# Five y pairs prepared in the key sweep, gates on GpSimd, and three more MLP steps by seven products

## Chip, core, metric

The kernel runs on one core of a Trainium2 chip. The metric is device time in microseconds (us) of one execution. The engines are named as in the profile: PE (TensorE matmuls), PEld (its weight loads), DVE (VectorE), ACT (ScalarE), POOL (GpSimd), SP (SyncE, which here only issues DMAs).

## The reference, cut to what matters

```python
# x: 2048 x 576, 32 heads of 18, F = 4608
g = sigmoid((x * gate_w).sum(-1, keepdims=True))
q, k, v = split(x @ wqkv);  phi = where(t > 0, t + 1, exp(t)) + 1e-6
a = ((phi(q) @ (phi(k)^T v)) / (phi(q) . sum(phi(k)) + 1e-6)) @ wo      # linear attention
y = layernorm(x);  b = gelu(y @ w1 + b1) @ w2 + b2                      # MLP, tanh gelu
out = g * a + (1 - g) * b
```

## The kernel before

All products run in fp32r: an operand is kept as a rounded high part (an ACT copy) and a low residue (a DVE subtraction), and two or three of the products of these parts are accumulated in PSUM.

**Key sweep.** Tokens are cut into 16 tiles of 128. For each tile the sweep forms keys and queries, their feature maps, and adds to the sum of keys times x. Each tile has three numbered moments, 3n, 3n+1 and 3n+2, at which listed jobs are put into the engines' queues; "step 16" below is such a moment. Jobs run in the order written, engine by engine. The gates (`gates_in`, `gates_act`, `gates_out`) turn a few columns of sums into sigmoid and 1/sqrt(variance); `share_moments` stores mean and 1/sqrt for later broadcast by a DMA that POOL issues. A *y pair* is the MLP's input for two tiles, laid out for the seven-product scheme: `load_pair` (SP) reads moments and transposed x, `normal_pair` and `sum_pair` (DVE) normalise and combine, `split_pair` (ACT, DVE) rounds seven parts, `store_pair` (SP) writes them to DRAM. The table `Y_JOBS` says at which step each is put. Four pairs, all of the first token half, are made in the sweep, and the four of the second half later, during the MLP, by `make_y`.

**Middle.** `project_values(t)` makes five row blocks of the weight `wp` on PE; each is copied by ACT and its residue made by DVE. `normalize(i, ...)` divides the queries of tile i (part 0: reduction and reciprocal, part 1: one scaling on DVE), `tail_q` copies their tail on ACT. Then `attend` handles the 16 tiles.

**MLP.** 36 steps: 18 chunks of w1 and w2 for the first token half (k = 0 to 17), then 18 for the second. The *up* part of a step is seven products of seven matmuls of 512 columns, tile `ps<-y,wa` or `ps<-y,wb`. The *down* part, tile `ps<-region,h`, comes one step later in two forms. Plain (`plain_unit`): 8 units of 12 matmuls of 288 columns, 96 in all. By seven products (`one_of_seven`, steps in the set `SEVEN`): 14 units of 6 matmuls, 84 in all, for which sums of w2's quarters (tile `fresh`, 4 of 288 columns) and of h (tile `u`, 4 of 512 columns) are needed, on DVE or POOL by the set `ON_DVE`, and more rounding of both. A step that is also in `FIVES` keeps one product in a buffer of its own, which takes copies by ACT and fewer additions by DVE than a step that is in `SEVEN` alone. In the first half w1 must be summed and rounded too, and the y pairs be made; the second half reads w1's rounded parts back.

A planner at the end of the program lists all these operations with costs and due times, and writes them out engine by engine; `TUNED` holds its parameters, `HEAR` what it adds for the time from one engine to another. Its numbers order the instructions and no more.

```python
def sum_w2(n, eng):
    to, x0, x1 = ((T3, B22, B12), (T1, B12, B11), (T2, B22, T1), (T4, B21, T2))[n]
    eng.tensor_tensor(out=of(to), in0=of(x0), in1=of(x1), op=OP.subtract)
```

Of the kernel before, what the change touches and what calls it, by code (L numbers as in the profile page):

```python
# [33 lines left out]
MOMENTS = ((0, 2), (2, 4), (4, 6), (6, 8), (8, 16))  # L34
# [42 lines left out]
Y_JOBS = ((13, (16, 16, 17, 17), (18, 18, 19, 19), (18, 19, 20, 21)), (20, (22, 22, 23, 23), (25, 25, 27, 27), (25, 26, 28, 29)), (27, (31, 31, 32, 32), (33, 33, 34, 34), (34, 35, 35, 36)), (35, (37, 37, 38, 38), (39, 39, 41, 41), (40, 42, 43, 44)))  # L77
# [49 lines left out]
def tile_gated_mix(ctx: ExitStack, tc: tile.TileContext, x, xm, xe, wm, we, wvm, wve, wo, um, ue, w2, b1, b2, gw, out):  # L127
# [33 lines left out]
    dve.memset(ones, 1.0)  # L161
    tiny = keep.tile([P, 1], F32, name="tiny")
# [200 lines left out]
    def gates_in(b):  # L363
        own, ve, _, _ = gate_parts(b)
        dve.tensor_copy(mr[b][:, 0], nmean[:, own])
        dve.tensor_scalar(ve, sumsq[:, own], 1 / D, EPS_LN, op0=OP.mult, op1=OP.add)

        dve.tensor_scalar(g[:, own], gsum[:, own], -87.0, None, op0=OP.max)

    def gates_act(b):  # L370
        own, ve, _, rstd = gate_parts(b)
        act.activation(g[:, own], g[:, own], AF.Exp, scale=-1.0)
        act.activation(rstd, ve, AF.Sqrt)
        if MOMENTS[b][1] < NT:
            act.activation(tiny, ones[:, 0:1], AF.Exp)

    def gates_out(b):
        own, ve, vr, rstd = gate_parts(b)
        dve.tensor_scalar(g[:, own], g[:, own], 1.0, None, op0=OP.add)
        dve.reciprocal(g[:, own], g[:, own])  # L380
        dve.tensor_scalar(omg[:, own], g[:, own], -1.0, 1.0, op0=OP.mult, op1=OP.add)
        dve.reciprocal(rstd, rstd)

        dve.tensor_mul(vr, rstd, rstd)
        dve.tensor_mul(vr, vr, ve)
        dve.tensor_scalar(vr, vr, -0.5, 1.5, op0=OP.mult, op1=OP.add)
        dve.tensor_mul(rstd, rstd, vr)
# [43 lines left out]
    def split_pair(sup, j, part, stage, width=2):  # L431
# [4 lines left out]
        act.activation(to[:, :, 0:3], src, AF.Copy)  # L436
        dve.tensor_sub(to[:, :, 3:5], src[:, :, 0:2], raw(to[:, :, 0:2]))
# [123 lines left out]
    jobs = {n: [] for n in range(3 * NT)}  # L561
# [15 lines left out]
    for b, n in enumerate((9, 13, 22, 28)):  # L577
        at(n, gates_in, b)
        at(n + 1, gates_act, b)
        at(n + 2, gates_out, b)  # L580
        at(n + 2, share_moments, b)

    for j, (loaded, normal, added, parts) in enumerate(Y_JOBS):
# [3 lines left out]
        for m, when in enumerate(added):  # L587
            at(when, sum_pair, 0, j, m)
# [1055 lines left out]
```

## Time and profile before

| | us |
|---|---|
| median of 3 runs (lowest to highest) | 1095.16 (1095.01 to 1095.65) |
| the profiled execution, its own time | 1096.17 |
| its span, first to last instruction | 1094.5 |
| PE busy in it | 1086.3 (99%) |
| DVE busy | 922.4 (84%) |
| ACT busy | 691.3 (63%) |
| POOL busy | 236.2 (22%) |
| granted TensorE clock | 1.0 throughout |

The profile is of one execution. What lies between its time and its span (1.67 us) is outside the instructions. Busy shares are means over stages that differ: in the first half of the MLP, DVE is far busier than its mean.

### The profile page before, as it was taken

What the parts mean: (1) busy time and instruction counts of PE and PEld (TensorE: products, weight loads), DVE (VectorE), ACT (ScalarE), POOL (GpSimd) and SP (SyncE); (2) the same over time, 40 slices, a digit from 0 to 9 for tenths busy, and PEclk for the clock granted to TensorE, in tenths of its full rate; (3) what the DMA queues carried; (4) which work ended last, traced back from release to release, by engine and by line L of the source; (5) the groups of instructions that cost most, each with busy time, mean ns of one, the idle gap of its engine ahead of it and who ended that gap; (6) DMA issues with size and microseconds to landing.
All of it is one profiled execution on the core that took longest, in us unless ns stands there. A gap on an engine that the chain in (4) does not pass through costs nothing.

```text
span 1094.5 us, 18650 instructions
## 1 busy us (share of the span) xinstructions
PE 1086.3 (99%) x6712; PEld 996.6 (91%) x6712; DVE 922.4 (84%) x1558; ACT 691.3 (63%) x1235; POOL 236.2 (22%) x232
## 2 busy tenths in 40 slices
PE   9999999999999999999999999999999999999998
PEld 8999999999898889988889988989899999999898
DVE  4568786896799999899999997988887888878888
ACT  6677766454667887777877876455555555455552
POOL 2111113431123232332111202121122211221110
PEclk9999999999999999999999999999999999999999
DMA  6466772745745665764556559574444445444432
GB/s 179 135 87 190 172 218 101 278 178 191 249 156 188 196 203 185 239 209 169 194 184 220 191 197 396 170 252 118 135 148 118 130 119 148 131 122 118 133 102 87
DMA packets 109006, 189.72 MB, mean 173 GB/s; under 512 B 8940, under 2 KB 68604, under 8 KB 104818
## 3 DMA queue, kind: packets, MB, share of 16 engines
q1 hardware_dynamic: 108002, 187.78, 53.7%
q8 instruction: 53, 0.87, 0.3%
q10 hardware_dynamic: 720, 0.74, 0.2%
q14 instruction: 39, 0.32, 0.1%
q0 software_dynamic: 192, 0.01, 0.0%
HBM read 121.70 MB, written 66.80 MB: 172 GB/s over the span
## 4 chain that ended last, share of the span: by engine, by line
PE 92%; DVE 3%; DMA 3%; ACT 1%; issue 0%; SPq 0%; ACTq 0%; DVEq 0%
PE ps L120 92%; DVE accs L120 1%; DMA accs<-moments 1%; DMA yd<-ystage 1%; DMA s<-in_wm 0%; DVE h L120 0%; DMA ystage<-late_acc 0%; DMA fresh<-in_ue 0%; DMA s<-in_we 0%; DVE wa L120 0%; DVE region L120 0%; DVE ystage L120 0%; DVE wb L120 0%; DVE fresh L120 0%; ACT u L120 0%
## 5 line engine op out<-in xcount | busy, mean ns | idle before, releaser
L120 PEld LDWEIGHTS ps<-region,h 128*128 128x128 f32 x3072 | 437.5, 188 | 30.2 <-ACT ps L120 4.7
L120 PE MATMUL ps<-region,h 128*128 128x288 f32 x3072 | 456.8, 295 | 0.8 <-DVE accs L120 0.7
L120 DVE TENSOR_TENSOR accs<-ps,accs 128x576 f32<-128x576 f32 x330 | 246.1, 753 | 60.7 <-PE ps L120 53.9
L120 PE MATMUL ps<-y,wa 128*128 128x512 f32 x1008 | 257.6, 392 | 0.0
L120 PEld LDWEIGHTS ps<-y,wa 128*128 128x128 f32 x1008 | 180.8, 188 | 30.5 <-ACT ps L120 0.2
L120 POOL TENSOR_TENSOR fresh<-fresh 128x288 f32<-128x288 f32 (+1 forms) x128 | 117.1, 918 | 409.5 <-DVE accs L120 144.5
L120 PE MATMUL ps<-y,wb 128*128 128x512 f32 x756 | 199.2, 393 | 0.4 <-ACT u L120 0.4
L120 DVE TENSOR_TENSOR h<-u,h 128x512 fp32r<-128x512 f32 x240 | 165.4, 702 | 8.7 <-ACT u L120 8.7
L120 PEld LDWEIGHTS ps<-y,wb 128*128 128x128 f32 x756 | 133.8, 188 | 21.1 <-ACT u L120 0.6
L120 PE MATMUL ps<-y 128*128 128x288 f32 (+2 forms) x950 | 133.9, 297 | 2.2 <-DVE wp L120 1.1
L120 PEld LDWEIGHTS ps<-y 128*128 128x128 f32 (+1 forms) x950 | 129.8, 188 | 4.4 <-DVE wp L120 1.8
L120 ACT ACTIVATE region<-fresh 128x576 fp32r<-128x576 f32 (+1 forms) x132 | 81.2, 625 | 73.9 <-PE ps L120 73.3
L120 ACT ACTIVATE ps<-ps 128x576 f32<-128x576 f32 (+1 forms) x127 | 78.6, 621 | 45.0 <-PE ps L120 21.5
L120 POOL TENSOR_TENSOR u<-u 128x512 f32<-128x512 f32 x44 | 57.1, 1298 | 193.2 <-DVE h L120 54.8
L120 DVE TENSOR_TENSOR region<-fresh,region 128x576 fp32r<-128x576 f32 (+1 forms) x132 | 94.3, 727 | 1.1 <-ACT region L120 1.1
L120 ACT ACTIVATE u<-ps 128x512 f32<-128x512 f32 x73 | 43.0, 589 | 68.2 <-PE ps L120 68.2
L120 ACT ACTIVATE h<-u 128x512 fp32r<-128x512 f32 x128 | 73.4, 621 | 9.9 <-DVE u L120 5.5
L120 ACT ACTIVATE h<-u,b1s 128x512 fp32r<-128x512 f32 x73 | 52.6, 722 | 42.2 <-DVE u L120 42.1
L120 PE MATMUL ps<-wp,qt 128*128 128x288 f32 x448 | 63.0, 297 | 0.0
L120 DVE TENSOR_TENSOR u<-ps,u 128x512 f32<-128x512 f32 x74 | 50.4, 683 | 13.6 <-PE ps L120 12.7
L120 PEld LDWEIGHTS ps<-wp,qt 128*128 128x128 f32 x448 | 59.8, 188 | 0.0
L120 DVE TENSOR_TENSOR u<-u 128x512 f32<-128x512 f32 x84 | 58.0, 691 | 1.7 <-POOL u L120 1.1
(139 smaller groups left out, 1044.8 us busy)
## 6 DMA issues: line engine op xcount, KB each, us to landing
w1d<-wa SPq DMA_DIRECT2D x17, 1280.0 KB
wa<-w1d SPq DMA_DIRECT2D x68, 320.0 KB
fresh<-in_w SPq DMA_DIRECT2D x70, 288.0 KB
y<-yd SPq DMA_DIRECT2D x14, 1280.0 KB
w1d<-wb SPq DMA_DIRECT2D x17, 960.0 KB
wb<-w1d SPq DMA_DIRECT2D x51, 320.0 KB
yd<-ystage SPq DMA_DIRECT2D x28, 320.0 KB
fresh<-in_um SPq DMA_DIRECT2D x64, 128.0 KB
```

The costliest lines, as they stand in the source:

```text
L120: self.last = self.tc.keep_in_program_order(op(*args, **kwargs))
```

## The change

It makes the first pair of the second token half in the sweep as well, so that five pairs stand there, one every six steps, and `make_y` makes three; splits `split_pair` into a high and a low part with steps of their own; moves the gates' arithmetic from DVE to POOL, with powers in place of reciprocals and square root, so that ACT's only function there is Exp; puts steps 0, 6 and 13 into `SEVEN` (and 6, 13 and 17 into `FIVES`, 16 out of it); lets each sum of w1 and w2 choose its engine apart; changes the planner's costs and parameters; and issues tile 1's scaling and its tail behind the copy of wp's fourth row block.

```diff
-MOMENTS = ((0, 2), (2, 4), (4, 6), (6, 8), (8, 16))
+MOMENTS = ((0, 2), (2, 4), (4, 6), (6, 8), (8, 10), (10, 16))
...
-Y_JOBS = ((13, (16, 16, 17, 17), (18, 18, 19, 19), (18, 19, 20, 21)), (20, (22, 22, 23, 23), (25, 25, 27, 27), (25, 26, 28, 29)), (27, (31, 31, 32, 32), (33, 33, 34, 34), (34, 35, 35, 36)), (35, (37, 37, 38, 38), (39, 39, 41, 41), (40, 42, 43, 44)))
+Y_JOBS = ((9, 14, (16, 16, 17, 17), (18, 18, 19, 19), (18, 19, 19, 20), (19, 20, 20, 21)), (15, 20, (22, 22, 23, 23), (24, 24, 25, 25), (24, 25, 25, 26), (25, 26, 26, 27)), (21, 26, (28, 28, 29, 29), (30, 30, 31, 31), (30, 31, 31, 32), (31, 32, 32, 33)), (27, 32, (34, 34, 35, 35), (36, 36, 37, 37), (36, 37, 37, 38), (37, 38, 38, 39)), (33, 38, (40, 40, 41, 41), (42, 42, 43, 43), (42, 43, 43, 44), (43, 44, 44, 45)))
...
-SEVEN = set([1, 2, 3, 4, 5, 7, 8, 9, 10, 11, 12, 14, 15, 16, 17, 18, 19, 20, 21, 22, 23, 24, 25, 26, 27, 28, 29, 30, 31, 32, 33, 34])
+SEVEN = set([0, 1, 2, 3, 4, 5, 6, 7, 8, 9, 10, 11, 12, 13, 14, 15, 16, 17, 18, 19, 20, 21, 22, 23, 24, 25, 26, 27, 28, 29, 30, 31, 32, 33, 34])
...
-FIVES = set([1, 2, 3, 4, 5, 7, 8, 9, 10, 11, 12, 14, 15, 16])
+FIVES = set([1, 2, 3, 4, 5, 6, 7, 8, 9, 10, 11, 12, 13, 14, 15, 17])
...
+HEAR_NS = {"PE": 155, "ACT": 65, "DVE": 65, "POOL": 110, "DMA": 300}
...
     def gates_act(b):
-        own, ve, _, rstd = gate_parts(b)
+        own = gate_parts(b)[0]
         act.activation(g[:, own], g[:, own], AF.Exp, scale=-1.0)
-        act.activation(rstd, ve, AF.Sqrt)
-        if MOMENTS[b][1] < NT:
-            act.activation(tiny, ones[:, 0:1], AF.Exp)
 
     def gates_out(b):
         own, ve, vr, rstd = gate_parts(b)
-        dve.tensor_scalar(g[:, own], g[:, own], 1.0, None, op0=OP.add)
-        dve.reciprocal(g[:, own], g[:, own])
...
+        n = ve.shape[1]
+        pool.tensor_scalar(omg[:, own], g[:, own], 1.0, None, op0=OP.add)
+        pool.tensor_tensor(out=g[:, own], in0=omg[:, own], in1=powers[:, 0:1].to_broadcast([P, n]), op=OP.pow)
...
+        pool.tensor_tensor(out=rstd, in0=ve, in1=powers[:, 1:2].to_broadcast([P, n]), op=OP.pow)
...
-    for b, n in enumerate((9, 13, 22, 28)):
-        at(n, gates_in, b)
-        at(n + 1, gates_act, b)
-        at(n + 2, gates_out, b)
-        at(n + 2, share_moments, b)
...
+    for pair, (gated, loaded, normal, added, high, low) in enumerate(Y_JOBS):
+        sup, j = divmod(pair, TPB)
+        at(gated, gates_in, pair)
+        for step in (gates_act, gates_out, share_moments):
+            at(gated + 1, step, pair)
...
+        at(loaded, load_pair, sup, j)
...
     project_values(2)
+    project_values(3)
     normalize(1, (1,))
+    project_values(4)
     tail_q(1)
-    project_values(3)
-    project_values(4)
...
     def make_y():
...
-        for j in range(TPB):
+        for j in range(len(Y_JOBS) - TPB, TPB):
```

Three places show what moves. First PE at the start of the MLP, before: 49 up matmuls of step 0, then those of step 1 with step 0's down matmuls (`region,h`) among them.

```order
L120 MATMUL ps<-y,wa 128x512 x28
L120 MATMUL ps<-y,wb 128x512 x21
L120 MATMUL ps<-y,wa 128x512 x28
L120 MATMUL ps<-region,h 128x288 x12
L120 MATMUL ps<-y,wb 128x512 x7
L120 MATMUL ps<-region,h 128x288 x24
L120 MATMUL ps<-y,wb 128x512 x7
```

The same place in the change:

```order
L120 MATMUL ps<-y,wa 128x512 x28
L120 MATMUL ps<-y,wb 128x512 x21
L120 MATMUL ps<-y,wa 128x512 x25
L120 MATMUL ps<-region,h 128x288 x6
L120 MATMUL ps<-y,wa 128x512 x3
L120 MATMUL ps<-y,wb 128x512 x4
L120 MATMUL ps<-region,h 128x288 x6
```

Units of 6 stand where units of 12 stood. Over the program the matmuls of this tile go from 3072 to 3036, all others keep their number, and the stretches of up matmuls between down matmuls go from 298 to 285.

Second, DVE in the middle, before: `wp` residues are the row blocks, `accs<-accs,den` is the scaling of a tile's queries (the first here is tile 1's), `den` rows are part 0 of `normalize`.

```order
L120 TENSOR_TENSOR wp<-ps,wp 128x576 x2
L120 SCALAR_TENSOR_TENSOR accs<-accs,den 128x576
L120 TENSOR_TENSOR wp<-ps,wp 128x576 x2
L120 TENSOR_REDUCE den<-qz 128x32
L120 TENSOR_TENSOR den<-den,den_2182 128x32
```

In the change:

```order
L120 TENSOR_TENSOR wp<-ps,wp 128x576 x3
L120 SCALAR_TENSOR_TENSOR accs<-accs,den 128x576
L120 TENSOR_TENSOR wp<-ps,wp 128x576
L120 TENSOR_REDUCE den<-qz 128x32
L120 TENSOR_TENSOR den<-den,den_2238 128x32
```

The fourth block's residue now stands ahead of the scaling. On ACT five `wp` copies stand in a row, where three stood ahead of tile 1's tail and two behind.

Third, POOL in the sweep, before: `pks` is the running sum of the keys, the DMA stores a pair's moments.

```order
L120 TENSOR_TENSOR pks<-pks,k 128x576
L120 DMA moments_116<-mr_110 128x4x1
L120 TENSOR_TENSOR pks<-pks,k 128x576 x2
L120 DMA moments_117<-mr_111 128x4x1
L120 TENSOR_TENSOR pks<-pks,k 128x576 x3
```

In the change, the first pair's operations behind ACT's Exp and their DMA (three more, on mean, variance and gate sum, stand ahead of the Exp):

```order
L120 TENSOR_SCALAR omg<-g 128x2
L120 TENSOR_TENSOR g<-omg,powers 128x2
L120 TENSOR_TENSOR mt<-omg,g 128x2
L120 TENSOR_SCALAR mt<-mt 128x2
L120 TENSOR_TENSOR g<-g,mt 128x2
L120 TENSOR_SCALAR omg<-g 128x2
L120 TENSOR_TENSOR mr_113<-mt,powers 128x2
L120 TENSOR_TENSOR mt<-mr_113 128x2
L120 TENSOR_TENSOR mt<-mt 128x2
L120 TENSOR_SCALAR mt<-mt 128x2
L120 TENSOR_TENSOR mr_113<-mr_113,mt 128x2
L120 DMA moments_120<-mr_113 128x4x1
```

Fourteen small POOL operations per pair stand ahead of the DMA, eleven of them behind ACT's Exp.

From the end of attention to the first weighing of the first token half's output, the orders also count, before and in the change: DVE additions from PSUM into `accs` 133 and 140, residues of h 121 and 128, sums of w2 32 and 41, sums of h 36 and 40, residues of w2 66 and 72, sums of w1 28 and 32, merges of `ps` into `u` 40 and 39; POOL sums of h 20 and 28, of w2 20 and 27, of w1 36 and 32.

## Rows read from the trace of the kernel before

**Rows 1.** The page: busy time by engine, and the chain that ended last.
```profile
PE 1086.3 (99%) x6712; PEld 996.6 (91%) x6712; DVE 922.4 (84%) x1558; ACT 691.3 (63%) x1235; POOL 236.2 (22%) x232
...
PE 92%; DVE 3%; DMA 3%; ACT 1%; issue 0%; SPq 0%; ACTq 0%; DVEq 0%
```

**Rows 2.** Waits of PE: total us, times, longest us.
```profile
PE ps L120 <- DVE wp L120: 1.1, 1, 1.1
...
PE ps L120 <- DVE accs L120: 0.7, 1, 0.7
PE ps L120 <- ACT u L120: 0.4, 1, 0.4
```

**Rows 3.** Busy time by stretch: PE, PEld, DVE, ACT, POOL, clock, DMA, GB/s.
```profile
50.00:195.00 145.00, 145.00 (x976) 138.78 (x975) 107.63 (x236) 102.38 (x225) 26.00 (x20) 1.00 0.59 153
345.00:650.00 305.00, 304.50 (x1801) 273.18 (x1800) 292.67 (x495) 237.81 (x395) 75.78 (x70) 1.00 0.58 196
720.00:1090.00 370.00, 370.00 (x2219) 336.45 (x2220) 310.58 (x469) 195.20 (x322) 71.05 (x75) 1.00 0.44 130
```

**Rows 4.** Timeline of PE: a short and the longest stretch of down matmuls.
```profile
301.09 1.74 PE L120 MATMUL ps<-region,h 128*128 128x288 f32 x12
...
1076.35 14.43 PE L120 MATMUL ps<-region,h 128*128 128x288 f32 x108
```

**Rows 5.** Timelines of PE, ACT and DVE in the middle stage.
```profile
191.99 7.99 PE L120 MATMUL ps<-y 126*128 126x288 f32 x54
...
201.67 3.99 PE L120 MATMUL ps<-y 128*128 128x288 f32 x28 [1.14 <-DVE wp L120]
...
199.98 0.31 ACT L120 ACTIVATE tail<-accs 128x128 f32<-128x128 f32 x1 [2.00 <-DVE accs L120]
200.19 1.17 ACT L120 ACTIVATE wp<-ps 128x576 fp32r<-128x576 f32 x2
...
198.68 1.26 DVE L120 SCALAR_TENSOR_TENSOR accs<-accs,den 128x576 f32<-128x576 f32 x1
200.86 1.42 DVE L120 TENSOR_TENSOR wp<-ps,wp 128x576 fp32r<-128x576 f32 x2 [0.92 <-ACT wp L120]
```

**Rows 6.** Groups by form: busy us, mean ns, idle us before.
```profile
L120 DVE TENSOR_TENSOR accs<-ps,accs 128x576 f32<-128x576 f32 x330 | 246.1, 753 | 60.7 <-PE ps L120 53.9 <-ACT u L120 3.4
L120 DVE TENSOR_TENSOR h<-u,h 128x512 fp32r<-128x512 f32 x240 | 165.4, 702 | 8.7 <-ACT u L120 8.7
L120 POOL TENSOR_TENSOR fresh<-fresh 128x288 f32<-128x288 f32 x92 | 80.4, 874 | 307.0 <-DMA fresh<-in_w 113.7 <-DVE accs L120 112.5 <-DVE fresh L120 25.7
...
L120 POOL TENSOR_TENSOR u<-u 128x512 f32<-128x512 f32 x44 | 57.1, 1298 | 193.2 <-DVE h L120 54.8 <-ACT u L120 53.6 <-DVE accs L120 29.1
...
L120 DVE TENSOR_TENSOR accs<-accs 128x384 f32<-128x384 f32 x32 | 18.5, 577 | 0.3
...
L120 DVE TENSOR_TENSOR fresh<-fresh 128x288 f32<-128x288 f32 x32 | 15.4, 480 | 0.0
...
L120 DVE TENSOR_TENSOR ystage<-accs,ystage 128x256 fp32r<-128x256 f32 x28 | 11.8, 420 | 0.0
```

**Rows 7.** Tile fresh on POOL: duration ns min/median/max, first and last start.
```profile
L120 POOL TENSOR_TENSOR fresh<-fresh x128: 802/815/2951, 291.1 to 1046.0; 128x288 f32<-128x288 f32 x92, 128x384 f32<-128x384 f32 x36
```

**Rows 8.** Key sweep: timelines of SP, DVE, PE, POOL, and one DMA's landing.
```profile
62.95 0.34 SPq L120 DMA_DIRECT2D accs<-moments  x1
...
72.70 3.81 DVE L120 TENSOR_TENSOR accs<-accs 128x768 f32<-128x768 f32 x4
...
50.74 3.90 PE L120 MATMUL ps<-y 128*128 128x288 f32 x28
...
61.94 3.90 PE L120 MATMUL ps<-y 128*128 128x288 f32 x28
...
3.36 0.73 POOL L120 TENSOR_SCALAR_AFFINE_SELECT accs<-accs 126x126 f32<-126x126 f32 x2
...
moments<-mr POOLq DMA_DIRECT2D x4, 2.0 KB, 10.2
```

More of the change, by code (lines that the diff above doesn't have):

```diff
@@ L161, in tile_gated_mix @@
     dve.memset(ones, 1.0)
+    powers = keep.tile([P, 2], F32, name="powers")
+    pool.memset(powers[:, 0:1], -1.0)
+    pool.memset(powers[:, 1:2], -0.5)
     tiny = keep.tile([P, 1], F32, name="tiny")
@@ L429, in tile_gated_mix, with split_pair, high_pair @@
     ys = {}
-    def split_pair(sup, j, part, stage, width=2):
+    def split_pair(*args):
+        high_pair(*args)
+        low_pair(*args[:3])
+    def high_pair(sup, j, part, stage, width=2):
         m0, m1 = width * part, min(width * part + width, 7)
@@ L436, in split_pair, with low_pair @@
         act.activation(to[:, :, 0:3], src, AF.Copy)
+    def low_pair(sup, j, part):
+        _, _, src, to = ys[sup, j, part]
         dve.tensor_sub(to[:, :, 3:5], src[:, :, 0:2], raw(to[:, :, 0:2]))
@@ L558, in tile_gated_mix @@
     y_stages.append(y_place.rearrange("p (m s n) -> p m s n", m=2, s=5))
-    jobs = {n: [] for n in range(3 * NT)}
+    jobs = {n: [] for n in range(3 * NT + 3)}
     def at(n, f, *args):
@@ L576, in tile_gated_mix @@
     at(40, load_wo)
[L577 to L584 removed]
+    for pair, (gated, loaded, normal, added, high, low) in enumerate(Y_JOBS):
[3 more added lines that the diff above has]
+            at(gated + 1, step, pair)
         for n, when in enumerate(normal):
[L586 removed]
+            at(when, normal_pair, sup, j, n // 2, n % 2)
         for m, when in enumerate(added):
[L588 to L592 removed]
+            at(when, sum_pair, sup, j, m)
+        for part, when in enumerate(high):
+            at(when, high_pair, sup, j, part, lambda part=part: y_stages[part])
+        for part, when in enumerate(low):
+            at(when, low_pair, sup, j, part)
+            at(when, split_tails, sup, j, part)
+            at(min(when + 1, 3 * NT + 2), store_pair, sup, j, part)
+        at(loaded, load_pair, sup, j)
     def run(n):
@@ L647, in tile_gated_mix @@
     projected(late[0], QUERY)
+    run(3 * NT)
     queries_out(late[0])
@@ L650, in tile_gated_mix @@
     moments_of(end)
+    run(3 * NT + 1)
     for part in range(2):
         add_products(end, part)
+    run(3 * NT + 2)
     pz = [ps[:, 6 + half, :HALF] for half in range(2)]
@@ L909, in tile_gated_mix @@
     COST = {ACT: (91, 0.838, 97), DVE: (70, 1.0425, 84), POOL: (250, 2.19, -78)}
-    HEAR = {PE: 155, ACT: 33, DVE: 33, POOL: 78, DMA: 30}
+    HEAR = HEAR_NS
+    EACH = {"up": (226.8, (6.3, 9.3, -2.7, 4.3, 9.3, 1.5, 5.5, 4.2)), "down": (131.9, (0, 3, -1, -2, 7, 1, 2, 3, -6, 1, 0, 1))}
     class Op:
@@ L1051, in sum_on @@
     def sum_on(what, k, m=0):
-        own = ((what, k, m) in ON_DVE) != ((m, k < NCHUNK) in DVE_SUMS)
+        own = (what, k, m) in ON_DVE
         return (DVE, dve) if own else (POOL, pool)
@@ L1128, in make_w2 @@
             for n in range(4):
[L1129 removed]
+                engine, eng = sum_on("w2", k, n)
                 op(engine, lambda n=n, eng=eng: sum_w2(n, eng), HALF, needs=[("w2raw", k)] + ([("w2sum", k, n - 1)] if n else []),
@@ L1445, in tile_gated_mix, with plan @@
     assert len(in_order) == len(ops)
-    def plan(lag, late, slop, slack, guard, ahead, second=None):
-        second = second or (lag, late, slop, slack, guard, ahead)
+    def plan(lag, late, slop, slack, guard, ahead, second, hold, wait):
         slot, due = {o: n for n, o in enumerate(ups)}, {}
@@ L1471, in plan, with streams @@
         port_at, moved, landed = {e: 0 for e in port_until}, 0.0, []
-        next_up, next_down, shift = 0, 0, 0.0
+        next_up, next_down, shift, run = 0, 0, 0.0, ["", 0]
+        def streams(o):
+            n = round(o.ns / (231.7 if o.by[0] == "up" else 132.3))
+            each, more = EACH[o.by[0]]
+            at_ = run[1] if run[0] == o.by[0] else 0
+            return n, n * each + sum(more[at_:at_ + n])
         def offer(o):
@@ L1520, in choose @@
                     if ta is not None and tb is not None:
-                        if tb <= ta + 100:
+                        if tb <= ta + 100 and not (run[0] == "up" and run[1] < hold and behind < wait and ta <= free[PE]):
                             ta = None
@@ L1550, in plan @@
             s, _, o = min(picks, key=lambda x: x[:2])
-            e, t = o.engine, s + o.tail
+            e, t, ns = o.engine, s + o.tail, o.ns
             if e == PE:
+                n, ns = streams(o)
+                t += ns - o.ns
+                run[:] = o.by[0], n + (run[1] if run[0] == o.by[0] else 0)
                 shift = s - nominal[o]
@@ L1557, in plan @@
                         late, slop, slack, guard = second[1:5]
+                        hold, wait = second[6:8]
                 else:
@@ L1580, in plan @@
             else:
-                free[e] = s + o.ns
+                free[e] = s + ns
             if o.port:
```

34 lines of the change are left out of this document (14 added, 20 removed).

## The prediction

> **What bounds the kernel now.** I read the page first: PE is busy 99% of the span, and the chain that ended last is PE for 92% [rows 1]. A busy PE could still be a waiting one, so the waits of PE come next: they hold one wait of 1.1 us on the residue of `wp`, one of 0.7 on DVE's additions into `accs`, and one of 0.4 on an ACT copy [rows 2]; nothing larger stands there. The busy time by stretch then shows who is near to making PE wait. In the key sweep (50 to 195 us) PE has no idle time, DVE is busy 107.63 of 145 us and ACT 102.38, so both have room. In 345 to 650 us, inside the MLP's first half, PE is busy 304.50 of 305 us, but DVE is busy 292.67, which leaves it 12.3 us. In the second half (720 to 1090 us) PE is full and DVE has 59 of 370 us free [rows 3]. So the kernel lasts as long as PE has matmuls, and DVE nearly stops it in one stage. What the change is worth is what it takes off PE, unless DVE, with POOL, takes it back there.
>
> **The change part by part**
>
> *Matmuls.* Three down steps go from 96 to 84 matmuls, 36 fewer in all, as the order counts too. A stretch of 108 such matmuls lasts 14.43 us and one of 12 lasts 1.74 [rows 4]; the difference, 12.69 us for 96 matmuls, is 0.132 us each, free of the modelled end. 36 x 0.132 = 4.75 us. These are full stretches on an engine that has no gap, so the whole of it is on the path. The clock is granted at its upper level, 2.4 GHz, throughout [rows 3].
>
> *Alternations.* Up and down stretches alternate 13 times less. By the same two rows a short stretch costs 1.74 - 12 x 0.132 = 0.15 us beyond its matmuls and the long one 14.43 - 108 x 0.132 = 0.17, so an alternation costs next to nothing. I take 0.1 us, between 0 and 0.3.
>
> *The fourth row block.* PE waits 1.14 us ahead of 201.67, for DVE [rows 5]. The chain behind it: DVE scales tile 1 until 199.94; ACT's copy of the tail, at 199.98, waited 2.00 us for that; behind it in ACT's queue stand the copies of blocks 4 and 5 from 200.19, and behind the first of them DVE's residue from 200.86 [rows 5]. In the change neither the scaling nor the tail stands ahead. The 54 value matmuls end at 199.98, at most, and block 4 ends 6 of 54 matmuls, 0.9 us, earlier: about 199.1. Copy and residue take half of 1.17 and half of 1.42, about 0.6 and 0.7 us: done at 200.4, when PE, which ran dry at 201.67 - 1.14 = 200.53, still has its transposes. So the wait goes nearly whole; I take 1.1 of it. What is late next: the scaling, now behind block 4, ends at about 201.7, and is wanted by PE's transposes of tile 1 behind 28 matmuls that begin now at 201.67 and last 3.99 us [rows 5]; block 5's residue comes 0.1 to 0.2 us later than now and is read no sooner. Nothing takes the wait's place that I can see. Bounds: 0 and 1.4.
>
> *The fifth pair in the sweep.* On DVE a pair costs 3.81 us of normalising [rows 8], four sums of 0.577, and fourteen roundings, the larger kind 0.42 [rows 6]: 3.8 + 2.3 + 5.9 = 12.0 us at most. The sweep has 37 us of DVE idle [rows 3], and gives up the gates' operations on DVE as well as ACT's square roots. It costs nothing in time while the order leaves the pair's operations between the tiles' own. If that cover were gone, DVE's queue would hold the keys' feature maps behind it.
>
> *Gates on POOL.* Eleven operations of two columns stand behind Exp. No row shows a power. Bounds from POOL's rows: two selections over 126 columns take 0.73 us, so 0.37 each [rows 8], and a sum over 288 columns takes 0.80 at the least [rows 7], which two columns should not reach. Eleven times 0.37 is 4 us, eleven times 0.80 is 8.8; I take 0.3 each, near the selection, so 3.3 us. A tile takes 61.94 - 50.74 = 11.2 us, a step 3.7 [rows 8]. The DMA is put at one step behind the gates and the load that waits for it four steps later, 14.9 us; the DMA lands 10.2 us after its issue [rows 8]. That leaves 4.7 us, or 0.43 us per operation, before SP waits at all, and then DVE's normalising still stands two steps behind the load, where before, first pair, it came 72.70 - 62.95 = 9.8 us behind it with no wait of DVE [rows 8]. Behind SP's waiting load stand loads of x tiles, which are issued tiles ahead. So I cost it at nothing.
>
> *The MLP's first half.* Its extra work on DVE, from the counts of the order: 7 additions (753 ns), 7 residues of h (702), 9 sums of w2 (480), 4 sums of h less one merge (about 700), and 10 others, no row of which I quote, between 480 and 700, taken at 600: 5.3 + 4.9 + 4.3 + 2.1 + 6.0 = 22.6 us; the moved pair takes off 12.0 [rows 6, 8]. On POOL 8 sums of h (1298 ns) and 7 of w2 (874) come in, 4 of w1 go, at least 874 each: 10.4 + 6.1 - 3.5 = 13.0 us [rows 6]. Two of the three steps, 6 and 13, lie in 345 to 650 us. There DVE gets 15.1 - 12.0 = 3.1 us more, POOL 8.7, and the stage is 3.2 us shorter. If all of POOL's work ran beside DVE's without stopping it, 6.3 of DVE's 12.3 us would be used: no wait. If it all kept DVE from working, 15.0 would be wanted: a lack of 2.7 us, which PE would wait. A sum of w2 on POOL takes 815 ns at the median and 802 at the least, but one took 2951 [rows 7]: mostly neither stops the other. I take 0.5 us, nearer to the lower end.
>
> The Trainium skill's page "SBUF — State Buffer", section "Who interferes with whom", says that a DVE instruction with two SBUF inputs contends with a GpSimd instruction that reads SBUF, one fully blocking the other. This case's 2951 ns beside a median of 815 fits it. By that rule, taken as if it held for all of POOL's work, the last term would be 2.7 us and the sum 1091.8.
>
> *The second half.* POOL's sums of w2 move to DVE there (33 by the order's count, x 0.48 = 16 us), which has 59 us idle [rows 3, 6]: nothing.
>
> **The sum**, against the profiled execution's own 1096.17 us (span 1094.5 and 1.67 around it): 1096.17 - 4.75 - 0.1 - 1.1 + 0.5 = 1090.7. That execution is 1.0 us above the median of the runs, 1095.16, so the runs should give 1089.7.
>
> **The rivals**
>
> *DVE and POOL become the bound.* The 12.3 us of DVE's idle time in 345 to 650 us may be no room at all, but waits that any order has. Then the added 3.1 + 8.7 = 11.8 us of work on the two engines lands on PE as far as it can't be hidden. Half of it, 5.9, gives 1089.7 - 0.5 + 5.9 = 1095.1, no change. For: DVE is 96% busy there. Against: PE waited little over 1 us in the whole MLP beside that DVE, and POOL has 229 of the 305 us free [rows 2, 3].
>
> *Slower: POOL's powers are late.* Place: SP's load of a pair's moments and, behind it, DVE's normalising in the sweep. If an operation took 1.5 us, the chain would take 16.5, 11.8 us beyond the 4.7 of room. Perhaps 1 us is to spare behind the load, and DVE's 37 us of idle time are 7.4 for each of five pairs, so PE would wait some 3.4 us per pair: 17 us, 1106.7. SP begins to wait at 0.43 us per operation; slower than before means 1.5 us lost per pair, 9.9 beyond the room, 1.3 us per operation. Against: no small POOL row is above 0.4.
>
> *The wait at wp only moves.* PE would then run dry at the first `attend`, or at block 5: 1.1 us back, 1090.8.
>
> *The waits in the MLP go too.* With the new order the 0.7 and 0.4 us [rows 2] and the 0.5 vanish: 1088.1.
>
> **How the numbers follow.** Forecast with the small terms as they are or somewhat off: 0.52, 1088.5 to 1091.5. MLP's waits gone: 0.13. Wait at wp only moved: 0.10. DVE and POOL bound: 0.18, most of it between 1092 and 1096, a third at or above 1093. Powers late: 0.04. What I have not thought of, on the slow side: 0.03. A measurement of this kernel tells 0.2%, 2.2 us, from no change, so faster means below 1093.0 and slower above 1097.4. Faster: 0.52 + 0.13 + 0.10 + 0.11 = 0.86. Slower: powers late 0.04, and 0.03 from the others. The rest, 0.07, is no change. The range takes the bounds of the terms below (no lack, both waits gone, 1.4 for wp): 1087.0, and reaches up to 1093.0.
>
> **What would show it.** Right: 3036 matmuls of `region,h`, and PE's busy time less by some 5 us; no wait on DVE's `wp`; in 50 to 195 us PE still full; PE's waits in the MLP no more than about 2 us in all; DVE in the first half above its present share. Wrong: PE idle in 345 to 650 us on DVE's `h`, `region` or `accs`, or on POOL's `u` (the first rival); DVE idle ahead of its 768-column operations for SP's loads (the second); a wait of about 1 us near 204 us (the third). The forecast fails if those waits pass 3 us.

## The result, and the profile after

The changed kernel takes 1098.56 us (median of 9 runs, 1095.71 to 1100.44), the kernel before, run beside it, 1095.49 (1095.01 to 1096.30). The ratio is 1.0027, 95% interval 1.0016 to 1.0037: slower by 0.27%, where 1089.7 and faster was forecast. The profiled execution took 1099.61 us, its span 1097.9.

The page after: busy time, and the chain that ended last.

```profile
PE 1084.0 (99%) x6676; PEld 992.7 (90%) x6676; DVE 943.8 (86%) x1558; ACT 694.1 (63%) x1236; POOL 271.1 (25%) x307
...
PE 80%; DVE 9%; DMA 4%; ACT 2%; issue 2%; POOL 1%; SPq 1%; ACTq 0%; DVEq 0%; POOLq 0%
```

PE has its 36 matmuls less, but holds 80% of the chain in place of 92% [rows 1]. The waits of PE after (us in total, times, longest) answer to [rows 2]:

```profile
PE ps L120 <- DVE k L120: 6.0, 3, 2.9
...
PE ps L120 <- DVE accs L120: 1.0, 2, 0.6
```

The waits on `k`, the keys' feature map, are new. The same stretches as in [rows 3], and one more, where the granted clock is at half, 1.2 GHz:

```profile
50.00:195.00 145.00, 138.85 (x902) 131.05 (x901) 107.55 (x192) 91.89 (x208) 53.28 (x85) 0.99 0.69 171
345.00:650.00 305.00, 304.85 (x1799) 274.10 (x1798) 303.10 (x517) 248.00 (x411) 77.85 (x74) 1.00 0.55 187
720.00:1090.00 370.00, 368.94 (x2202) 333.59 (x2201) 319.49 (x485) 197.69 (x323) 62.77 (x58) 1.00 0.43 129
```

```profile
182.00:185.50 3.50, 3.50 (x18) 3.50 (x17) 2.96 (x6) 3.49 (x5) 1.16 (x1) 0.51 0.45 173
```

The loss is in the sweep: PE is idle 6.2 of its 145 us, and in the MLP's full stage only 0.15 us beside a DVE with 1.9 us left. PE's timeline shows where (the first row is cut off by the end of its view, at 148 us):

```profile
146.61 1.60 PE L120 MATMUL ps<-y 128*128 128x288 f32 x10 [0.52 <-DVE k L120]
```

```profile
170.22 3.97 PE L120 MATMUL ps<-y 128*128 128x288 f32 x28 [2.65 <-DVE k L120]
...
180.82 5.50 PE L120 MATMUL ps<-y 128*128 128x288 f32 x28 [2.86 <-DVE k L120]
...
200.46 7.99 PE L120 MATMUL ps<-y 126*128 126x288 f32 x54
...
209.18 3.98 PE L120 MATMUL ps<-y 128*128 128x288 f32 x28 [0.19 <-DVE wp L120]
```

The 28 matmuls at 180.82 take 5.50 us in place of 3.90, in the stretch at half clock, behind the longest wait. The stretch of 54 value matmuls starts at 200.46, before at 191.99 [rows 5]: 8.5 us late. The next row started at 201.67 before, so 1.0 comes back at `wp`, where 1.14 had been waited and now 0.19. From that row to the end of the span it was 1094.5 - 201.67 = 892.8 us and is 1097.9 - 209.18 = 888.7: 4.1 back in attention and MLP. 8.5 - 1.0 - 4.1 = 3.4, the difference of the spans. So the forecast gains came nearly whole, 5.1 us of 5.45, and the sweep lost 8.5: 6.0 of waits on `k`, 1.6 at half clock, the rest small.

The queues behind the two long waits (POOL, SP, DVE, ACT, in that order):

```profile
145.54 0.87 POOL L120 DMA_DIRECT2D moments<-mr  x1 [0.29 <-POOL mr L120]
```

```profile
157.58 0.62 SPq L120 DMA_DIRECT2D accs<-moments  x1
...
165.43 2.65 SPq L120 DMA_DIRECT2D wot<-in_wo  x2
168.18 0.51 SPq L120 DMA_DIRECT2D yd<-y  x1
```

```profile
165.58 1.95 DVE L120 TENSOR_TENSOR accs<-accs 128x768 f32<-128x768 f32 x2 [3.89 <-DMA accs<-in_xe]
```

```profile
178.90 0.52 ACT L120 ACTIVATE y<-accs 128x384 fp32r<-128x384 f32 x1 [1.99 <-DMA yd<-y]
```

The fifth pair's moments are stored at 145.54; SP, which waits for them, loads from 157.58, 12.0 us later; DVE stands 3.89 us for the pair's operands, with `k` behind it in its queue. Then ACT waits 1.99 us for the fourth pair's last store, which SP issued at 168.18 behind the late pair and behind 1.4 MB of `wo`. Behind ACT's copy stand the exponentials for the next `k`.

### The profile page after: what moved, and what is told of

Read it like the earlier page. It is cut to its first block, busy times and chain, and to the rows that moved or that the text cites. A ratio compares the mean times of both kernels' runs of the same rounds, so it can differ in the third digit from the quotient of the medians.

```text
span 1097.9 us, 18660 instructions
## 1 busy us (share of the span) xinstructions
PE 1084.0 (99%) x6676; PEld 992.7 (90%) x6676; DVE 943.8 (86%) x1558; ACT 694.1 (63%) x1236; POOL 271.1 (25%) x307
## 4 chain that ended last, share of the span: by engine, by line
PE 80%; DVE 9%; DMA 4%; ACT 2%; issue 2%; POOL 1%; SPq 1%; ACTq 0%; DVEq 0%; POOLq 0%
PE ps L120 80%; DVE accs L120 3%; DVE h L120 2%; DMA fresh<-in_w 1%; DVE region L120 1%; DMA yd<-y 1%; DVE u L120 1%; DMA moments<-mr 1%; SPq L120 1%; DVE wa L120 1%; DVE fresh L120 1%; DMA accs<-in_xe 1%; DVE wb L120 0%; DVE ystage L120 0%; DMA s<-in_we 0%
## 5 line engine op out<-in xcount | busy, mean ns | idle before, releaser
L120 PEld LDWEIGHTS ps<-region,h 128*128 128x128 f32 x3036 | 431.9, 188 | 29.5 <-ACT ps L120 2.2
L120 PE MATMUL ps<-region,h 128*128 128x288 f32 x3036 | 449.7, 295 | 1.7 <-DVE accs L120 1.0
L120 DVE TENSOR_TENSOR accs<-ps,accs 128x576 f32<-128x576 f32 x340 | 251.4, 752 | 32.7 <-PE ps L120 25.8
L120 DVE TENSOR_TENSOR h<-u,h 128x512 fp32r<-128x512 f32 x249 | 174.8, 727 | 8.2 <-ACT u L120 7.1
L120 POOL TENSOR_TENSOR fresh<-fresh 128x288 f32<-128x288 f32 (+1 forms) x94 | 83.3, 888 | 319.4 <-DMA fresh<-in_w 62.6
L120 POOL TENSOR_TENSOR u<-u 128x512 f32<-128x512 f32 x66 | 87.3, 1323 | 285.2 <-DVE h L120 83.4
L120 ACT ACTIVATE region<-fresh 128x576 fp32r<-128x576 f32 (+1 forms) x138 | 84.7, 623 | 86.7 <-PE ps L120 85.4
L120 ACT ACTIVATE ps<-ps 128x576 f32<-128x576 f32 (+1 forms) x137 | 85.1, 622 | 50.5 <-PE ps L120 31.1
L120 ACT ACTIVATE h<-u 128x512 fp32r<-128x512 f32 x140 | 81.7, 621 | 4.9 <-DVE u L120 4.3
L120 DVE TENSOR_TENSOR accs<-accs 128x768 f32<-128x768 f32 (+1 forms) x64 | 49.6, 779 | 10.6 <-DMA accs<-in_xe 9.9
```

The lines of the kernel that those rows point to most:

```text
L120: self.last = self.tc.keep_in_program_order(op(*args, **kwargs))
```

## The experiments

Each experiment below was forecast before it ran; the indented text is that forecast. "Kernel 7" is the kernel of experiment 7. Two theories at first. A: in SP's and POOL's queues DMAs stand too late, the moments' store ahead of SP's load and `wo` ahead of the fourth pair's store; moving them mends it. B: the gates' operations on POOL cost, wherever they stand. The first forecasts add C: a fifth pair is more than DVE's queue holds.

**1. Gates of the later pairs three steps earlier**

```diff
-(15, 20, ...  (21, 26, ...  (27, 32, ...  (33, 38, ...
+(12, 20, ...  (18, 26, ...  (24, 32, ...  (30, 38, ...
```

> The changed kernel with the gates of pairs 2 to 5 put three steps earlier (steps 12, 18, 24, 30 in place of 15, 21, 27, 33), all else alike. Theory A (late loads: the moments land late, SP's load of a pair waits for them, DVE's normalising waits for the load, the keys' feature map waits behind it in DVE's queue, and PE behind that): the waits of PE on DVE's k near 146 and 167 us go, 3.2 us of the 6.0; the one near 178 us, behind ACT's copy that waits for the store of pair 4's last part, shrinks because SP is no longer held before that store; with it the stretch at half clock behind the two waits (1.5 us). So 1093 to 1095. Theory B (the small POOL operations themselves slow DVE down, wherever they stand): nothing gained, 1098. Theory C (a fifth pair is more than DVE's queue holds in the last tiles): nothing gained either, the waits stand at DVE with no idle time of DVE before its 768-column operations.

Measured 1106.47 us, ratio 1.0105 (1.0079 to 1.0131): far slower, and none of the three has it. Its SP, POOL and DVE rows at the second pair, and the DMA's rate behind them (last two columns of the window: DMA share, GB/s):

```profile
91.26 0.97 SPq L120 DMA_DIRECT2D accs<-in_xm  x1
...
94.65 1.13 SPq L120 DMA_DIRECT2D accs<-in_xe  x2
```

```profile
95.16 0.87 POOL L120 DMA_DIRECT2D moments<-mr  x1 [0.29 <-POOL mr L120]
```

```profile
99.46 1.93 DVE L120 TENSOR_TENSOR accs<-accs 128x768 f32<-128x768 f32 x2
104.54 1.95 DVE L120 TENSOR_TENSOR accs<-accs 128x768 f32<-128x768 f32 x2 [3.15 <-DMA accs<-in_xe]
```

```profile
100.00:105.00 5.00, 5.00 (x35) 4.72 (x35) 1.82 (x3) 2.70 (x8) 0.00 (x0) 1.00 0.78 69
```

SP waits no more, but the next pair's store now starts just as this pair's loads are issued. They arrive when it lands, and the DMAs move 69 GB/s with 0.78 of their time taken.

**2. wo much earlier**, at step 24

```diff
-    at(40, load_wo)
+    at(24, load_wo)
```

> The changed kernel with the load of wo (1.4 MB) put at step 24 in place of 40, so that it no longer stands in SP's queue between pair 4's stores, all else alike. Theory A: the wait near 178 us goes (2.9 us, ACT's copy of a pair's last part waited 2.0 us for the store of the part before it, which SP issued behind the load of wo), the one near 167 us stays at 2.7; the clock stays up: 1094 to 1095.5. If the store is late because SP was held by the moments alone, the wait stays and the time is 1098.

Measured 1105.80, ratio 1.0097 (1.0084 to 1.0110), outside what either reading had. PE's wait on `k` there is 11.3 us at once, ahead of 134 us: DVE waits 6.9 and 6.1 us for the third pair's loads, and `wo`, issued at 102.29, now stands ahead of them in SP's queue.

**3. Both**

> Both edits: gates of pairs 2 to 5 three steps earlier and the load of wo at step 24. Theory A: PE is full from 50 to 195 us, no wait on DVE's k, clock 1.0, and what the change takes off PE shows: 1098.6 - 6.0 - 1.5 - 0.8 of small waits = 1090 to 1091. Theories B and C: 1096 to 1098.

Measured 1103.16, ratio 1.0078 (1.0066 to 1.0090), again outside what any theory had: DVE still waits 3.8 to 4.9 us at a time for loads.

**4. Gates on DVE and ACT again**, at the change's steps, the store one step later

```diff
-        for step in (gates_act, gates_out, share_moments):
-            at(gated + 1, step, pair)
+        at(gated + 1, gates_act, pair)
+        for step in (gates_out, share_moments):
+            at(gated + 2, step, pair)
```

> The changed kernel with the gates computed as before (DVE, and Sqrt on ACT with its table loads), at the changed kernel's steps, moments stored one step later than there (two behind the gates). Theory A: what counts is when the moments land; before, the chain from Exp to the DMA took 3 us on DVE and ACT where it takes 4 to 6 on POOL, but the store stands one step later, so the load of pair 5 is still late: PE keeps more than half of its waits on k, 1096 to 1099. Theory B (POOL's operations slow DVE): the waits go, 1090 to 1092.

Measured 1095.10, ratio 0.9998 (0.9989 to 1.0007), between the theories. PE still waits 3.0 us near 175 us, and DVE 1.3 us for the fifth pair.

From 1 and 3 a further theory, D: a store of moments is slow, and while it is in flight the loads issued beside it are slow too. There is a right moment, neither the change's nor three steps ahead.

**5. Gates one step earlier**

```diff
-(15, 20, ...  (21, 26, ...  (27, 32, ...  (33, 38, ...
+(14, 20, ...  (20, 26, ...  (26, 32, ...  (32, 38, ...
```

> The change with the gates of the pairs behind the first one step earlier (steps 14, 20, 26, 32 in place of 15, 21, 27, 33) and nothing else. Theory D: a store of moments by POOL takes 9 to 11 us, SP's next load waits for it, and while it is in flight the loads of a pair issued beside it come late. In the change it lands just as SP gets to the load or later; three steps earlier (the first experiment) it is in flight beside the loads of the pair before. One step earlier, about 3.7 us, it is clear of both: DVE's waits of 1.0 to 3.9 us ahead of its 768-column operations go to under 1 us, PE's waits on k near 146 and 170 us (0.5 and 2.7) go, the one near 181 us (2.9, with half the clock behind it) stays: 1094.5 to 1096. Rival: the gates' small operations on POOL disturb DVE wherever they stand: 1097.5 to 1100, and the DVE waits stay.

Measured 1092.37, ratio 0.9974 (0.9964 to 0.9983), faster than D had it (1094.5 to 1096). DVE waits 0.65 us once for the fifth pair's loads, and more than 0.2 nowhere else; PE's wait near 175 us is still 1.80 us, with 28 matmuls at half clock behind it. B falls: the same POOL operations, one step earlier, cost nothing visible.

**6. wo behind the fourth pair's last store**

```diff
-    at(40, load_wo)
+    at(41, load_wo)
```

> The change with the load of wo one step later, behind the fourth pair's last store in SP's queue in place of ahead of it. Theory D: that store lands some 9 us after its issue instead of 10.6 to 11, since 1.4 MB no longer stand ahead of it, so ACT's copy near 179 us does not wait 2.0 us for it, and PE's wait of 2.9 us near 181 us and the half clock behind it (1.6) go: 1094 to 1096, with the wait near 170 us (2.7) still there. Rival: the store is late from POOL's store of moments and the loads behind it, not from wo: the wait near 181 us stays at 2 us or more and the time at 1097 to 1099.

Measured 1093.78, ratio 0.9982 (0.9973 to 0.9991). ACT's wait for the store is gone. PE's near 176 us is still 1.95 us, since DVE is late from the fifth pair (1.7 us). So that wait has two causes, one behind the other. But D had the wait near 170 us stay at 2.7, and it is 0.33. The orders of this kernel and of the change are the same up to that load of `wo`, and yet here the fifth store is followed by SP's load after 8.2 us (12.0 in the change) and DVE waits 1.7 us (3.89):

```profile
145.57 0.87 POOL L120 DMA_DIRECT2D moments<-mr  x1 [0.29 <-POOL mr L120]
```

```profile
153.82 0.54 SPq L120 DMA_DIRECT2D accs<-moments  x1
```

So of the 4.8 us between the two medians, PE's trace gives `wo` about 0.9 (2.86 to 1.95). The rest arises ahead of the edit: the landing of the store, and what hangs on it, differs between executions of one order by several us. The change was timed once, and not again beside the kernels of these experiments, so what an edit is worth against it is rough.

**7. Both**

> Both of the last two edits together. Theory D: no wait of PE on k above 0.5 us is left and the sweep ends within 1.5 us of where it ended before: 1090 to 1092, which is the blind forecast. Rival, that the fifth pair is more than the sweep's DVE and ACT can carry: PE still waits 3 us or more on k in 100 to 195 us, 1094 or above.

Measured 1091.06 (5 runs, 1090.88 to 1093.69), ratio 0.9966 (0.9954 to 0.9979): faster than both kernels, the best here that computes the reference, and within D's range. C falls: the sweep carries five pairs with 0.8 us of wait on `k`. Its waits of PE, and the row that stood at 180.82 in the change:

```profile
PE ps L120 <- DVE accs L120: 0.9, 3, 0.4
PE ps L120 <- DVE k L120: 0.8, 1, 0.8
...
PE ps L120 <- DVE wp L120: 0.2, 1, 0.2
```

```profile
174.59 3.98 PE L120 MATMUL ps<-y 128*128 128x288 f32 x28 [0.78 <-DVE k L120]
...
192.75 7.97 PE L120 MATMUL ps<-y 126*128 126x288 f32 x54
```

**8. Kernel 4 with wo one step later**

> The change with the gates on DVE and ACT as before (at the change's steps, the store one step later) and the load of wo one step later. Theory D: the wait of 3.0 us near 175 us that was left with the gates on DVE goes: 1091 to 1093, little different from both edits with the gates on POOL, so the engine of the gates matters less than when the store is in flight. Rival, that the gates on POOL are what cost: this one is 2 us or more faster than the kernel with both edits.

Measured 1094.35 (11 runs, 1092.13 to 1096.49), ratio 0.9994 (0.9985 to 1.0003), outside what either had it. Its profiled execution is its fastest, with a span of 1090.4, 1.0 above that of kernel 7; PE waits 2.0 us near 176 us. Nothing here shows POOL's gates to be worse; but the two kernels also differ in when the store is issued (the fifth at 145.20 and 142.69), and why this one's runs stand 3.3 us above kernel 7's stays open.

**9. Kernel 1 with 16-byte elements**

```diff
-        pool.dma_start(moments[b].rearrange("a (t n) -> n (a t)", n=P), ...)
+        pool.dma_start(moments[b].rearrange("a m -> (a m)").rearrange("(n x) -> n x", n=P), ...)
```

> The first experiment again (gates of the later pairs three steps earlier, so that the store is in flight beside the loads of the pair before), but a store of moments writes one run of 16 bytes for each partition, 128 in all, in place of 512 single elements of 4 bytes. The moments then stand in another order in DRAM, so the pairs are normalised with wrong numbers; the work and its sizes are the same. If it is the number of small elements that holds the loads back: the store lands in about 3 to 5 us, DVE's waits of 3.1 to 4.7 us ahead of its 768-column operations go to under 1 us, and the time is 1091 to 1094. If it is that POOL issues the store, whatever its elements: the waits stay at 3 us or more and the time at 1104 to 1108.

Measured 1091.16, ratio 0.9967 (0.9954 to 0.9979). The store stands as in kernel 1, at 90.65 beside loads from 86.31 on, and DVE's four operations run through:

```profile
90.65 0.67 POOL L120 DMA_DIRECT2D moments<-mr  x1 [0.29 <-POOL mr L120]
```

```profile
94.80 3.81 DVE L120 TENSOR_TENSOR accs<-accs 128x768 f32<-128x768 f32 x4
```

```profile
96.00:101.00 5.00, 5.00 (x34) 4.69 (x34) 4.30 (x7) 3.23 (x10) 0.12 (x1) 1.00 1.03 399
```

399 GB/s against kernel 1's 69 behind the same point. Same queue, same issuer, same step: it is the 512 elements of 4 bytes. Whether they would be as slow in the queue of another engine, no run shows.

**10. Kernel 7 with four pairs in the sweep**

```diff
-Y_JOBS = (..., (32, 38, (40, 40, 41, 41), ...))
+Y_JOBS = (...)
```

> The kernel with both edits (gates one step earlier, wo one step later) with four pairs in the sweep, so that the fifth is made in the MLP again. By the prediction's stage sum the MLP's first half takes back 12.0 us of DVE's work where DVE has 2 to 3 us free in 345 to 650 us: PE waits on DVE there and the time is 1094 to 1101. Rival, that the order of the MLP hides a pair anyway, so that the fifth pair in the sweep buys nothing: 1090 to 1092.

Measured 1108.40, ratio 1.0117 (1.0104 to 1.0131), slower than either reading had it. PE's waits, and the full stage:

```profile
PE ps L120 <- ACT ps L120: 3.6, 5, 1.1
PE ps L120 <- ACT u L120: 3.2, 3, 2.5
PE ps L120 <- DVE h L120: 2.5, 1, 2.5
```

```profile
345.00:650.00 305.00, 297.36 (x1728) 263.01 (x1728) 301.75 (x511) 241.06 (x401) 73.22 (x71) 1.00 0.56 193
```

From the fourth row block to the end it takes 1106.4 - 199.91 = 906.5 us, in kernel 7 1089.4 - 201.47 = 887.9: the pair costs 18.6 us there, more than its 12.0 of DVE work. (The planner's numbers were left as for five pairs, so part may be theirs.)

**11. Kernel 7 with steps 0, 6 and 13 plain**

```diff
-SEVEN = set([0, 1, 2, 3, 4, 5, 6, 7, 8, 9, 10, 11, 12, 13, 14, ...
+SEVEN = set([1, 2, 3, 4, 5, 7, 8, 9, 10, 11, 12, 14, ...
```

> The kernel with both edits with steps 0, 6 and 13 plain again: 36 matmuls more, 3072 of region,h. By the prediction's step: 4.75 + 0.1 us more, less what DVE and POOL no longer make PE wait (0 to 1): 1095 to 1096. Rival, that the saved matmuls come back as waits in the MLP: 1091 to 1093.

Measured 1097.18 (1095.22 to 1100.98), ratio 1.0024 (1.0014 to 1.0034), 0.6% above kernel 7 and 1.2 us above its forecast. From the fourth row block (202.73) to the end of the span (1095.5) it takes 892.8 us: 4.8 more than in kernel 7, against 4.85 in the prediction's step (one execution of each). The other 1.3 us lie in the sweep, whose orders are those of kernel 7: PE's wait on `k` is 1.70 there in this execution, 0.78 in that of kernel 7.

**12. The kernel before with wp's new order alone**

```diff
     project_values(2)
+    project_values(3)
     normalize(1, (1,))
-    tail_q(1)
-    project_values(3)
     project_values(4)
+    tail_q(1)
```

> The kernel before with the order at wp alone (the fourth row block ahead of tile 1's scaling, its tail behind the fifth). By the prediction's step the wait of 1.14 us goes: 0.9 to 1.1 us faster, 1094.1 to 1094.4. Rival, that the wait only moves to the next reader: no change, 1095.2.

Measured 1094.48, ratio 0.9996 (0.9987 to 1.0005): too small for the timing to resolve. The trace is plainer: the wait on `wp` goes from 1.1 [rows 2] to 0.2 us, and no other takes its place there.

**13. The change with 16-byte elements, and nothing else** (the store's edit of 9)

> The change with nothing else altered than the store of moments: 128 runs of 16 bytes in place of 512 elements of 4 bytes (the moments then stand in another order in DRAM, so the pairs are normalised with wrong numbers; work and sizes are the same). If the elements alone cost: the store lands in 2 to 5 us, SP does not wait, DVE's and PE's waits near 146, 170 and 181 us go to about 1 us together, the half clock does not appear: 1090.5 to 1092. If the load of wo costs by itself: the wait near 181 us stays at 2 us or more: 1093.5 to 1096. If POOL's gates cost: 1097 or above.

Measured 1092.10 (11 runs, 1090.11 to 1094.30), ratio 0.9973 (0.9964 to 0.9982). One edit gives back about 6 us (6.5 by the two medians, 5.9 by the ratios to the kernel before, 1.0027 and 0.9973), as far as the change's single timing goes. The time is near what the first reading had; the wait near 181 us, here near 176, stays at 1.95 us, as the second had it. DVE's waits for loads shrink to 0.2 us, and no half clock appears. The stores' landing, of the change (four of its five; the fifth, followed by SP's load after 12.0 us, isn't in the view) and of this kernel:

```profile
DMA to landing us min/median/max: 8.3/9.4/10.1
```

```profile
DMA to landing us min/median/max: 1.8/2.8/3.0
```

SP's load of the fifth pair, which now waits for nothing, and what is left of `wo`, in ACT and PE:

```profile
153.84 0.42 SPq L120 DMA_DIRECT2D accs<-moments  x1
```

```profile
174.00 0.52 ACT L120 ACTIVATE y<-accs 128x384 fp32r<-128x384 f32 x1 [2.06 <-DMA yd<-y]
```

```profile
175.92 3.99 PE L120 MATMUL ps<-y 128*128 128x288 f32 x28 [1.95 <-DVE k L120]
```

**14. The kernel before with 16-byte elements**

> The kernel before with the same alteration of the store alone (again wrong numbers in the pairs, same work). Its trace shows no wait of DVE for the pairs' loads, so nothing should be won: 1094.5 to 1095.5. If the long store also costs elsewhere, unseen: below 1093.

Measured 1094.96, ratio 1.0001 (0.9992 to 1.0010): nothing. The same store was as slow before (10.2 us [rows 8]); there it had room.

**15. 16-byte elements with right numbers**: kernel 13, `wo` one step later, and DVE reading the moments in the order in which they then stand

```diff
+        if sup * TPB + j < len(Y_JOBS):
+            row = rows.rearrange("p a n -> p (a n)").rearrange("p (n x) -> p x n", x=4)[:, 2 * k + a:2 * k + a + 1].to_broadcast([P, 6, P])
```

> The change with the store of moments as 128 runs of 16 bytes, DVE's 768-column operations of the five pairs reading the moments at a stride of four numbers, and the load of wo one step later; gates where the change has them. If a strided read costs DVE nothing: its operations stay at 0.98 us, no wait above 0.5 us on the pairs' loads, no half clock: 1090 to 1092. If it costs: the operations take 1.3 us or more, 20 of them, 6 us of DVE's time that the sweep mostly hides: 1091 to 1095.

Measured 1101.47, ratio 1.0059 (1.0046 to 1.0073), beyond both ranges: the read costs, and the sweep doesn't hide it. DVE waits for no load, but its operation takes 1.56 us in place of 0.96; below, the group in this kernel and in kernel 7 (busy us, mean ns), and two of this kernel's waits of PE:

```profile
L120 DVE TENSOR_TENSOR accs<-accs 128x768 f32<-128x768 f32 x20 | 30.6, 1557 | 0.5
```

```profile
L120 DVE TENSOR_TENSOR accs<-accs 128x768 f32<-128x768 f32 x20 | 19.0, 961 | 0.8 <-DMA accs<-in_xe 0.2
```

```profile
85.80 4.01 PE L120 MATMUL ps<-y 128*128 128x288 f32 x28 [0.89 <-DVE accs L120]
...
184.60 5.50 PE L120 MATMUL ps<-y 128*128 128x288 f32 x28 [1.94 <-DVE k L120]
```

20 x 0.6 = 12 us more on a DVE with 37 us idle in the sweep [rows 3], and the kernel is 10.4 us slower than kernel 7; PE waits 8.4 us on DVE in the sweep. So the sweep's idle time on DVE is hardly room: four operations in a row hold up the `k` behind them.

## Why the prediction was wrong, step by step

**The step that failed** is "gates on POOL", costed at nothing, and with it "the fifth pair costs nothing". Its sum was 3.3 us of operations and 10.2 of landing, 13.5 against a distance of 14.9. At the fifth pair of the change the first operation starts at 139.71, the store at 145.54 and SP's load at 157.58: 5.8 and 12.0 us, 17.9 in all. Where SP waits for nothing (run 13) it loads at 153.84, so the real distance was 14.1 and the load came 3.7 us late. Both terms were too small, and the room that was to take up the rest wasn't there.

The operations. Three of the groups in the sweep after (busy us, mean ns):

```profile
L120 POOL TENSOR_TENSOR g<-omg,powers 128x2 f32<-128x2 f32 x5 | 4.4, 883 | 0.4
...
L120 POOL TENSOR_TENSOR mr<-mt,powers 128x2 f32<-128x2 f32 x5 | 4.2, 839 | 0.0
L120 POOL TENSOR_SCALAR mt<-mt 128x2 f32<-128x2 f32 x10 | 4.1, 405 | 0.9
```

The eleven operations' means add up to 4.9 us, 0.45 each and 0.53 with the gaps between them, where 0.43 was the room. The 0.3 taken was no bad price for POOL left alone: in the first pair, with DVE mostly idle beside it, the eleven take 3.0 us, and a power 0.7. In the later pairs they stand beside DVE's normalising of the pair before, and an operation that starts while DVE runs one on two operands in SBUF is often lengthened, to 0.9 us and a power to 1.5. The same operation in the first and the fifth pair, and what DVE ran beside the fifth's (the row merges two operations, the second ending at 143.94):

```profile
52.70 0.20 POOL L120 TENSOR_TENSOR mt<-mt 128x2 f32<-128x2 f32 x1
...
143.08 0.92 POOL L120 TENSOR_TENSOR mt<-mt 128x2 f32<-128x2 f32 x1
```

```profile
141.99 1.95 DVE L120 TENSOR_TENSOR accs<-accs 128x768 f32<-128x768 f32 x2 [1.97 <-DMA accs<-in_xe]
```

The prediction weighed DVE stopping POOL for the MLP, and not here. That only this lengthens them is read from the trace, not from an experiment.

The landing. 10.2 us came from the order before. In the change it goes from 8.3 to 12.0, and with the same order in run 6 the fifth is 8.2; why it differs so isn't shown.

What stands behind the load. I wrote that DVE's normalising "still stands two steps behind the load", as if that were room. Two steps are 7.5 us, and the loads take about 8: the fifth pair's from 157.58 to 165.58. Before, the first pair's stood 9.8 us behind [rows 8]. So any lateness of SP went to DVE, and from there to `k`. The rival of POOL's powers being late named the place and the order of waits, but had its price wrong: it asked for 1.3 us per operation, and 0.53 sufficed, since the landing was longer, the 1 us of room assumed behind the load wasn't there and DVE's idle 7.4 us per pair can hardly be drawn on (run 15).

What neither text nor rival had: the store's own slowness hinders the loads beside it (runs 1, 9). Its elements cost the change about 6 us (run 13, rough as said in run 6), and `wo`'s place about 1 by PE's waits (run 6, and kernel 5 against 7: 1.80 and 0.78); the 1.3 us between the times of kernels 5 and 7 lie within their intervals. With gates and `wo` both moved, 1091.06 stands 1.4 above the forecast, inside its range.

**Matmuls and alternations**: 4.85 forecast, 4.8 measured in one execution of each kernel (run 11). Right.

**The fourth row block**: 1.1 forecast, 0.95 in the trace, not resolved in the time (run 12). Right in kind, and the rival that the wait only moves did not come.

**The MLP's first half**: 0.5 of lack forecast, 0.15 of PE's idle time in the full stage. The size of the work was off: DVE rose by 10.4 us there in place of 3.1, POOL by 2.1 in place of 8.7 (the row of 345 to 650 against that of [rows 3]), since in that stretch POOL made six sums of w1 fewer and DVE nine more, and the moved pair took some 8 us off DVE there in place of 12.0. Their joint size, 12.5, came near the 11.8 forecast, so that the small wait agrees is in part luck. By the Trainium skill's page "SBUF — State Buffer", section "Who interferes with whom", taken for all of POOL's work, PE would have waited 2.7 us in the prediction's sum; no run here shows that wait, with DVE at 303.10 and POOL at 77.85 of the same 305 us.

**The fifth pair in the sweep** buys more than was said: with three more steps by seven products the MLP, as planned here, can't carry it (run 10, 18.6 us, of which part may be the planner's numbers).

**The rivals in the MLP** (DVE and POOL the bound; the waits gone) did not come.

**Slips in the working** that change nothing: the range's lower end, from its own terms, is 1087.8 (1087.6 with the bound of the alternations), not 1087.0; the sum with 2.7 us of lack is 1091.9, not 1091.8; and the list of PE's waits leaves out 1.1 us on `ones` and 0.8 on ACT's `y`, ahead of 50 us, which stand in the change too.

## To carry to other kernels

When a transfer is put close ahead of its reader, count the chain in full: producer's operations, issue, landing, the reader's load and its landing, and the distance that the order before had kept. An engine's idle time is room only where the order leaves it between the operations that someone waits for. A small operation on POOL has two prices here, alone and beside DVE's. And look at the element size of a small store before its bytes: 2 KB in 512 pieces cost some 6 us here (run 13).

## What the runs showed of the hardware

512 elements of 4 bytes took 8.3 to 11.4 us to land (the change and run 1; the change's fifth, by SP's load behind it, 12.0), 128 of 16 bytes 1.8 to 3.0 in run 13 and up to 5.4 in run 9, beside a pair's loads; the loads of SP's queue beside the first kind fell to 69 GB/s. The Trainium skill's page "DMA: Bandwidth & Descriptors", section "Why small descriptors are slow (HBM only)", tells of a fixed overhead for each packet and for each DMA operation's descriptors, which fits the first in kind, not worked out in size; that the loads of another queue arrive only when the store does, runs 1 and 9 show, without its cause.

An operation of two columns on POOL took 0.19 to 0.24 us (a power 0.69 to 0.73) in the first pair, and up to 0.92 (1.52) in the later ones, the long ones mostly beside a DVE operation on two operands in SBUF.

A DVE operation of 768 columns with one operand read at a stride of four 4-byte numbers took 1.56 us, with the same operand read at a stride of one 0.96. The Trainium skill's page "SBUF — State Buffer", section "Door 1: The DMA port swizzle", says that SBUF has lines of 16 bytes and that each access to a new line pays; every number lies in a new line here, and the trace agrees.

The clock fell to 1.2 GHz behind waits of PE of 1.80 to 3.05 us in the change (182 to 185.5 us) and in kernels 4, 5, 6 and 15, each time with some 1.6 us lost on 28 matmuls (5.50 in place of 3.90). In kernels 13 and 8 waits of 1.95 and 1.97 us, and in kernel 3 one of 2.11, had 28 matmuls of 3.98 or 3.99 us behind them, at the full clock. What decides it stays open.
